# Attention into a gated FFN: the last two pairs of token tiles one after the other, stores as outputs become whole, output-weight sums and fourth sums at other places in the order

## The chip, the cores and the metric

The kernel runs on one core of one Trainium2 chip. The time is device time of one launch in microseconds (us). The core has four compute engines that matter here, each with its own instruction stream: TensorE (PE: matmuls into PSUM), VectorE (DVE), ScalarE (ACT) and GpSimd (POOL). SyncE (SP) issues most of the DMAs. An engine runs its instructions in the order in which the program was recorded and waits on semaphores for other engines.

## The reference

```python
# q, k, v: (4, 8, 768, 64); centroids: (8, 16, 64)
q_assign = argmax(q_n @ c_n.T); k_assign = argmax(k_n @ c_n.T)
mask = q_assign[..., :, None] == k_assign[..., None, :]
attn = softmax(where(mask, scale * q @ k.T, -1e9))
x = (attn @ v).transpose(0, 2, 1, 3).reshape(3072, 512)
# w_gate, w_val: (512, 1536); w_out: (1536, 512)
gate = 1.0 / (1.0 + np.exp(-(x @ w_gate)))
val = x @ w_val
return gate * val @ w_out
```

## The kernel before

The program is recorded once, in one order, by a step counter: every step is one scores block of attention (transposed keys times queries, `do_scores`, exponential on ScalarE, then `do_av`), and in between each step takes some atoms of FFN work from `queue` (`ffn_run`) and background work that was planned for that step (`plan(name, step, f)`, `at`, `run_bg`). The numbers in the table `SCHED` override the planned step where a name is in it. Batches 0 to 3 follow each other; the FFN of a block of 384 tokens runs under the attention of what comes next. The second block of the last batch has no attention to run under: `ffn_block(xT, 384, 384, B - 1, True)` and `ffn_run(1e9)` stand at the end of the program.

A block of 384 tokens is three token tiles of 128. Its FFN is 12 blocks `fc` of 128 hidden units: `gate` (L529, four matmuls, then tanh on ScalarE) and `val` (L545, four matmuls, then on VectorE `hT = (th + 1) * v`, L550). g, v, scores and most other PSUM tiles come from `ring`, four banks in turn, so a bank is free only when its reader is through. Two further banks are in the pool `op`.

For batches 1 to 3 the output product is not done tile by tile (`plain_out`) but for pairs of tiles, with seven products in place of eight (Winograd's form of a 2 by 2 product). For a pair, the hidden units are in two halves of `HF` = 6 chunks and the output columns in two halves of `HD` = 256. `tok(b, t, f)` is half f of tile t. The sums of halves are made on VectorE: on the side of the hidden units by `Sums.make(i)` (four per pair: L626 to L632), and on the side of `w_out` once by `mix_wo(i, c)` (T1 to T4, each in two halves `c`, L276), planned as `wt{i}{c}`. T1 to T3 lie in the buffers `kheld`, `qheld`, `vheld`.

`product_out` takes the products in the order 1, 4, 6, 5, 7, 3, 2 over two banks, x (1, 6, 7, 2) and y (4, 5, 3). After each, VectorE adds the bank into the output tile `ob` (`plus`, L658), with product 1 copied by ScalarE (L662). Products 7 and 3 go on accumulating in the bank that 6 and 5 filled, after the addition has read it. The fourth sum, `make(4)`, written over the second, is needed by product 3. Tiles 0, 1 of a batch are a single pair (its 14 atoms go to `aside` and alternate with those of `queue`); tiles (3, 2) and (4, 5), the second block, are two pairs at once (`P_` = 2), side by side in the columns of a bank. Each finished output row is stored by SP (`store`, L502).

In the last block the two pairs also run side by side, after all 12 gate and val blocks: six products for both, then product 2 by `closing` in three pieces.

Of the kernel before, what the change touches and what calls it, by code (L numbers as in the profile page):

```python
# [8 lines left out]
FP = mybir.dt.float32  # L9
HP = mybir.dt.float16  # L10
AF = mybir.ActivationFunctionType
ALU = mybir.AluOpType
# [86 lines left out]
def kernel(  # L99
# [61 lines left out]
    def bank(n=512, dt=FP, name="bank"):  # L161
        return ring.tile([128, n], dt, tag="ring", name=name)
# [3 lines left out]
    def out_bank():  # L166
        taken["op"] += 1
        return op.tile([128, DM], FP, tag="o", name="o")
# [103 lines left out]
    def mix_wo(i, c):  # L272
        done.add(("wt", i, c))
        o, a, z = [(T1, B12, B11), (T3, B22, B12), (T2, B22, T1), (T4, B21, T2)][i]
        c = slice(3 * c, 3 * c + 3)
        DVE.tensor_tensor(o[:, c], a[:, c], z[:, c], ALU.subtract)  # L276
# [220 lines left out]
    def tok(b, t, f):  # L497
        return HB[b, t // 3][:, HF * f : HF * f + HF, bass.ts(t % 3, 128)]

    def store(src, b, c0, n, m=slice(0, DM)):  # L500
        def f():
            SP.dma_start(  # L502
                out=out[b * S : (b + 1) * S].rearrange("(p c) m -> p c m", c=NCH)[
                    :, c0 : c0 + n, m
                ],
                in_=src,
            )

        d_ = SCHED.get("sd", 0)
        if d_ > 0 and b < B - 2:  # L510
            at(step_no[0] + d_, f)
        else:
            f()

    def ffn_atoms(xT, t0, n, b, final=False):
        blk = t0 // 384
        gv = []
        cost = NDC * max(n, 80) / 2.4 + 3
        pairs = [] if b < PB else [(0, 1)] if blk == 0 else [(3, 2), (4, 5)]
        sm = {x: Sums(b, *x) for x in pairs}  # L520

        def gate(fc, st):
            def f():
                need(("w", fc // WQ, 0), *(("x", b, p, t0 // 128 + c) for p in range(NP) for c in range(n // 128)))
                if fc == 0:
                    HB[b, blk] = htp.tile([128, NFC, 384], HP, name="hT")
                g = bank(512, name="g")
                for dc in range(NDC):
                    PE.matmul(  # L529
                        out=g[:, 0:n], lhsT=wg[fc // WQ][:, dc, fc % WQ, :],  # L530
                        rhs=xT[:, dc, t0 : t0 + n],
                        start=(dc == 0), stop=(dc == NDC - 1),
                    )
                th = thp.tile([128, 384], FP, name="th")
                ACT.activation(th[:, 0:n], g[:, 0:n], AF.Tanh)  # L535
                st.append(th)

            return f

        def val(fc, st):  # L540
            def f():
                need(("w", fc // WQ, 1))
                w = bank(512, name="v")
                for dc in range(NDC):
                    PE.matmul(  # L545
                        out=w[:, 0:n], lhsT=wv[fc // WQ][:, dc, fc % WQ, :],
                        rhs=xT[:, dc, t0 : t0 + n],
                        start=(dc == 0), stop=(dc == NDC - 1),
                    )
                DVE.scalar_tensor_tensor(  # L550
                    HB[b, blk][:, fc, 0:n], st[0][:, 0:n], 1.0, w[:, 0:n], ALU.add, ALU.mult
                )
                for k, x in SUMS_AT[b >= PB, blk].get(fc, []):
                    sm[x].make(k)
                if fc == NFC - 1 and pairs and blk == 0:
                    aside.extend(product_out(b, [sm[(0, 1)]], False))

            return f

        for fc in range(NFC):  # L560
            st = []
            gv.append((cost, gate(fc, st)))
            gv.append((cost, val(fc, st)))
        outs = []
        if b < PB:
            for t in range(n // 128):
                outs += plain_out(b, blk, t)
        elif blk == 1:
            outs = product_out(b, [sm[x] for x in pairs], final)
        return gv + outs  # L570

    def plain_out(b, blk, t):
        OA = SCHED.get(f"oa{b}{384 * blk}", SCHED.get("oa", 4))
# [33 lines left out]
        },  # L607
    }

    class Sums:  # L610


        def __init__(self, b, t1, t2):
            self.b, self.t1, self.t2, self.of = b, t1, t2, {}

        def make(self, i):
            a1 = lambda f: tok(self.b, self.t1, f)
            a2 = lambda f: tok(self.b, self.t2, f)
            if i == 4:
                self.of[4] = self.of[2]  # L620
            else:
                t = sump.tile([128, HF, 128], HP, tag="sum", name="sum")
                self.of[i] = t
            o = self.of[i]
            if i == 1:
                DVE.tensor_tensor(o, a2(0), a2(1), ALU.add)  # L626
            elif i == 2:
                DVE.tensor_tensor(o, self.of[1], a1(0), ALU.subtract)
            elif i == 3:
                DVE.tensor_tensor(o, a1(0), a2(0), ALU.subtract)  # L630
            else:
                DVE.tensor_tensor(o, a1(1), o, ALU.subtract)  # L632

    def product_out(b, sums, final):


        P_ = len(sums)
# [42 lines left out]

        def end3():
            plus(st[C12], st["y"], st[C12])
            if final:
                store(st[C12], b, sums[0].t1, P_, slice(HD, DM))

        def end2():
            plus(st[C11], st["x"], st[C11])
# [31 lines left out]

            return f  # L720

        def closing(e, a, z):
            def f():
                o = bank(z - a, name="o_end")
                lhs = tok(b, sums[e].t1, 1)
                for c in range(HF):
                    PE.matmul(  # L727
                        out=o, lhsT=lhs[:, c, :], rhs=B21[:, c, a:z],
                        start=c == 0, stop=c == HF - 1,
                    )  # L730
                m = st["o1"][:, e, a:z]
                plus(m, o, m)
                store(m.unsqueeze(1), b, sums[e].t1, 1, slice(a, z))

            return f

        for k in range(6 if final else 7):
# [3 lines left out]
        if final:  # L741
            for e, a, z in ((0, 0, HD), (1, 0, HD // 2), (1, HD // 2, HD)):
                atoms.append((900, closing(e, a, z)))
        return atoms

    queue = []
# [118 lines left out]
    def plan(name, step, f):  # L865
        at(SCHED.get(name, step), f)
# [8 lines left out]
    def need(*names):  # L875
        for n in names:
            assert n in done, n
# [623 lines left out]
```

## Time and profile before

| | us |
|---|---|
| three runs | 324.08, 324.35, 324.59 |
| the profiled execution, its own time | 324.13 |
| its span, first to last instruction | 322.3 |
| TensorE, VectorE, ScalarE, GpSimd busy | 314.6, 226.4, 231.3, 108.6 |

Rows of the profile name the line of the kernel, the engine, the operation, and the tiles written and read, with the number of instructions in a row. In the timeline the first column is the start in us from the span's start, the second the duration of the group; brackets give the idle time of that engine before it, and what ended it. The ends of matmuls are modelled and overlap the next start, so a loss on TensorE is best read from start to start. PE is TensorE's matmul, PEld its weight load, SPq SyncE's queue. The granted clock of TensorE is full over the whole span.

### The profile page before, as it was taken

Reading aid. Unit: us, or ns where it says so; the run is one execution under the profiler, and the core shown is the slowest. Engines: PE = TensorE matmul, PEld = TensorE weight load, DVE = VectorE, ACT = ScalarE, POOL = GpSimd, SP = SyncE. Lnnn points to the kernel's source line nnn. Section 1 sums busy time; section 2 is a strip of 40 time slices with the busy share of each in tenths; the row PEclk is TensorE's granted clock in tenths of the full one; section 3 lists DMA queues with packets and bytes.
Section 4 is the critical chain, followed back from the end, with each engine's and each line's share of the span. In section 5 each row is a group of like instructions: output and inputs, shape, how many; then the busy total and the mean of one; then the engine's idle time right before and its main releaser. Section 6 shows DMA issues by size and latency. Waiting matters only on the chain.

```text
span 322.3 us, 9168 instructions
## 1 busy us (share of the span) xinstructions
PE 314.6 (98%) x3510; PEld 222.1 (69%) x3510; DVE 226.4 (70%) x588; ACT 231.3 (72%) x520; POOL 108.6 (34%) x145
## 2 busy tenths in 40 slices
PE   7999999999999999999999999999999999999995
PEld 5888666766766656666777687666777688566674
DVE  5899656777667997576879588676867356555655
ACT  6688988787898977877767866788777886332220
POOL 5887464154335275433143342523111111000000
PEclk9999999999999999999999999999999999999999
DMA  6999996738988677974694652952503112200103
GB/s 205 379 253 171 259 169 120 205 85 232 248 121 226 112 218 153 229 175 130 116 212 121 202 113 60 288 124 52 111 2 91 39 26 79 77 2 1 67 0 130
DMA packets 77835, 45.15 MB, mean 140 GB/s; under 512 B 56864, under 2 KB 75232, under 8 KB 77792
## 3 DMA queue, kind: packets, MB, share of 16 engines
q1 hardware_dynamic: 73824, 39.73, 48.2%
q0 software_dynamic: 3680, 4.72, 9.0%
q8 instruction: 27, 0.44, 0.6%
q14 instruction: 16, 0.13, 0.1%
q10 hardware_dynamic: 288, 0.13, 0.1%
HBM read 28.34 MB, written 6.29 MB: 107 GB/s over the span
## 4 chain that ended last, share of the span: by engine, by line
PE 91%; DVE 6%; issue 1%; ACT 1%; ACTq 0%; POOL 0%; DVEq 0%
PE g L529 19%; PE v L545 19%; PE sc L803 18%; PE o L713 12%; PE av L826 10%; PE o L583 4%; PE lg L434 2%; PE lg L421 1%; PE t_ps L1052 1%; PE oh_ps L1112 1%; DVE lgs L449 0%; DVE T L1065 0%; DVE vheld L276 0%; PE vs_ps L354 0%; PE o_end L727 0%
## 5 line engine op out<-in xcount | busy, mean ns | idle before, releaser
L808 ACT ACTIVATE es<-sc 128x384 f16<-128x384 f32 x384 | 174.7, 492 | 40.0 <-PE sc L803 30.7
L803 PE MATMUL sc<-T 128*128 128x384 f16 x384 | 117.8, 326 | 1.0 <-DVE lgs L449 0.6
L826 PEld LDWEIGHTS <-es 128*128 128x128 f16 x1152 | 81.4, 98 | 35.3 <-issue 0.2
L826 PE MATMUL av<-va,es 128*128 128x65 f16 x1152 | 97.6, 194 | 0.0
L550 DVE SCALAR_TENSOR_TENSOR hT<-th,v 128x384 f16<-128x384 f32 x96 | 53.1, 553 | 55.8 <-PE av L826 36.6
L529 PE MATMUL g<-xTb,wg 128*128 128x384 f16 x384 | 78.2, 326 | 0.1
L545 PE MATMUL v<-xTb,wv 128*128 128x384 f16 x384 | 78.1, 326 | 0.0
L535 ACT ACTIVATE th<-g 128x384 f32<-128x384 f32 x96 | 47.2, 492 | 32.8 <-PE g L529 13.7
L375 POOL TENSOR_TENSOR xp<-t,rec 128x384 f16<-128x384 f32 (+1 forms) x30 | 21.8, 728 | 100.4 <-DVE rec L372 49.9
L529 PEld LDWEIGHTS <-wg 128*128 128x128 f16 x384 | 37.2, 97 | 19.7 <-issue 0.4
L545 PEld LDWEIGHTS <-wv 128*128 128x128 f16 x384 | 37.4, 98 | 19.0
L803 PEld LDWEIGHTS <-T 128*128 128x128 f16 x384 | 37.1, 97 | 0.7 <-DVE T L1133 0.7
L1369 POOL TENSOR_TENSOR hl<-kraw,hl 128x384 f16<-128x384 f32 x22 | 20.2, 920 | 42.0 <-DVE hl L1368 19.6
L658 DVE TENSOR_TENSOR ob<-o,ob 128x256 f32<-128x256 f32 (+1 forms) x41 | 21.9, 547 | 8.8 <-PE o L713 8.1
L713 PEld LDWEIGHTS <-sum 128*128 128x128 f16 x216 | 20.9, 98 | 5.6 <-DVE sum L632 0.7
L1369 POOL TENSOR_TENSOR hl<-qraw,hl 128x384 f16<-128x384 f32 x22 | 20.7, 940 | 10.0 <-DVE hl L1368 9.7
L713 PE MATMUL o<-wo,hT 128*128 128x256 f16 x150 | 22.5, 272 | 0.0
L370 DVE TENSOR_TENSOR t<-av,sv 128x390 f32<-128x390 f32 (+1 forms) x30 | 14.4, 479 | 8.2 <-PE av L826 7.3
L583 PE MATMUL o<-wo,hT 128*128 128x512 f16 x72 | 19.9, 379 | 0.0
L713 PEld LDWEIGHTS <-hT 128*128 128x128 f16 x150 | 14.6, 97 | 3.7
L449 DVE TENSOR_REDUCE lgs<-lg 128x192 f32<-128x384 f32 x23 | 12.7, 550 | 2.8 <-PE lg L434 2.6
L322 POOL CAST va<-vraw 128x768 f16<-128x768 f32 x15 | 13.0, 868 | 2.6 <-DMA vraw<-in_v_dram 2.6
(143 smaller groups left out, 324.9 us busy)
## 6 DMA issues: line engine op xcount, KB each, us to landing
vraw<-in_v_dram SPq DMA_DIRECT2D x15, 384.0 KB, 4.8
kraw<-in_k_dram SPq DMA_DIRECT2D x14, 384.0 KB, 4.0
out_dram<-ob SPq DMA_DIRECT2D x19, 256.0 KB, 2.3
qraw<-in_q_dram SPq DMA_DIRECT2D x12, 384.0 KB, 4.3
wg<-in_moe_w_gate_dram POOLq DMA_DIRECT2D x2, 768.0 KB, 9.6
wv<-in_moe_w_val_dram POOLq DMA_DIRECT2D x2, 768.0 KB, 10.6
wo<-in_moe_w_out_dram POOLq DMA_DIRECT2D x2, 768.0 KB, 9.3
T<-ohT SPq DMA_DIRECT2D x44, 24.0 KB, 1.9
```

Source lines behind the costliest of these rows:

```text
L375: (eng or POOL).tensor_tensor(x, t[:, 0:nq, 0:64], bcast(rec[:, 0:nq], 64), ALU.mult)
L529: PE.matmul(out=g[:, 0:n], lhsT=wg[fc // WQ][:, dc, fc % WQ, :], rhs=xT[:, dc, t0 : t0 + n], start=(dc == 0), stop=(dc == NDC - 1),)
L535: ACT.activation(th[:, 0:n], g[:, 0:n], AF.Tanh)
L545: PE.matmul(out=w[:, 0:n], lhsT=wv[fc // WQ][:, dc, fc % WQ, :], rhs=xT[:, dc, t0 : t0 + n], start=(dc == 0), stop=(dc == NDC - 1),)
L550: DVE.scalar_tensor_tensor(HB[b, blk][:, fc, 0:n], st[0][:, 0:n], 1.0, w[:, 0:n], ALU.add, ALU.mult)
L583: PE.matmul(out=o, lhsT=HB[b, blk][:, fc, bass.ts(t, 128)], rhs=wo[fc // WON][:, fc % WON, :], start=(fc == 0), stop=(fc == NFC - 1),)
L658: plus = lambda dst, a, z: DVE.tensor_tensor(dst, a, z, ALU.add)
L713: PE.matmul(out=st[z][:, e], lhsT=a[:, c, :], rhs=rhs[:, c, :], start=start and c + e == 0, stop=c == HF - 1, skip_group_check=True,)
L803: PE.matmul(out=sc.rearrange("p (c t) -> p c t", t=128), lhsT=s["k"], rhs=s["q"], start=True, stop=True,)
L808: ACT.activation(es, sc, AF.Exp, scale=SCALE)
L826: PE.matmul(out=av[:, a0 + s["c0"] + i, :], lhsT=s["es"][:, bass.ts(i, 128)], rhs=VA[b, p][:, e, s["j"], :], start=(first and i == 0 and a ...
L1369: POOL.tensor_tensor(hl[:, :, 64:128], r, hl[:, :, 0:64], ALU.subtract)
```

## The change

Three things are changed.

1. The sums of output weights: `wt0`, `wt1`, `wt2` (both halves) are planned at steps 109 to 128 instead of 150 to 170. `wt3` keeps its steps.
2. In `product_out`, the fourth sum of each pair is recorded after the addition of product 6 instead of after that of product 5.
3. The last block has an order of its own, `closing`. The first pair's products 1, 4, 6 and 5 are recorded in halves between the gate and val atoms of blocks 7 to 11. Then come product 7 of pair a, products 1 and 4 of b, 3 of a, 6 and 5 of b, 2 of a, 7 and 3 of b, and 2 of b in two column halves. Pair a uses the two banks of `op`, pair b banks of the ring. Each store follows the last addition into its part of the output. Its sums come from a table of their own, `SUMS_LAST`: those that need hidden units 6 to 11 are made in two pieces, of five chunks at block 10 and of one at block 11, and the fourth sum has its own tile.

```diff
@@ ffn_atoms
+        when = SUMS_LAST if final else SUMS_AT[b >= PB, blk]
...
-                for k, x in SUMS_AT[b >= PB, blk].get(fc, []):
-                    sm[x].make(k)
+                for k, x, *c in when.get(fc, []):
+                    sm[x].make(k, *c)
...
+        if final:
+            return closing(b, gv, sm[(3, 2)], sm[(4, 5)])
         return gv + outs
+
+    def closing(b, gv, ma, mb):
+        ac, order = [], []
+        plus = lambda dst, a, z: DVE.tensor_tensor(dst, a, z, ALU.add)
+        def pair(m, bk):
...
+            def product(k, g=0, n=HF):
+                def f():
+                    z = {1: "a", 4: "d", 6: "x", 7: "x", 5: "y", 3: "y"}[k]
...
+                    mm(o, k, g, n, k not in (7, 3))
+                    if g + n < HF:
+                        return
+                    if k == 1:
+                        ACT.activation(C(0, 0), o, AF.Copy)
+                    elif k == 4:
+                        plus(C(1, 0), o, C(0, 0))
+                    elif k == 6:
+                        plus(C(0, 1), o, C(0, 0))
+                    elif k == 5:
+                        plus(C(1, 1), o, C(0, 0))
+                    elif k == 7:
+                        plus(C(1, 0), o, C(1, 0))
+                        plus(C(1, 1), o, C(1, 1))
+                        store(st["ob"][:, 1:2], b, m.t2, 1)
+                    else:
+                        plus(C(0, 1), o, C(0, 1))
+                        store(st["ob"][:, 0:1, HD:DM], b, m.t1, 1, slice(HD, DM))
...
+            def last(parts):
+                def f():
+                    for a, z in parts:
+                        o = bank(z - a, name="o_end")
+                        mm(o, 2, 0, HF, True, a, z)
+                        plus(st["ob"][:, 0, a:z], o, st["ob"][:, 0, a:z])
+                    store(st["ob"][:, 0:1, 0:HD], b, m.t1, 1, slice(0, HD))
...
+        pa, la = pair(ma, bank_a)
+        pb, lb = pair(mb, lambda z: bank(512, name="o_end"))
+        early = [pa(k, g, HF // 2) for k in (1, 4, 6, 5) for g in (0, HF // 2)]
...
+        early[0] = drained(early[0])
+        atoms = gv[:14]
+        for i, x in enumerate(gv[14:]):
+            atoms.append(x)
+            if i < len(early):
+                atoms.append((0.0, early[i]))
+        for f in (
+            pa(7), pb(1), pb(4), pa(3), pb(6), pb(5), la([(0, HD)]), pb(7), pb(3),
+            lb([(0, HD // 2), (HD // 2, HD)]),
+        ):
+            atoms.append((0.0, f))
+        return atoms
...
+    SUMS_LAST = {
+        1: [(1, (3, 2))], 5: [(2, (3, 2)), (3, (3, 2))], 6: [(3, (4, 5))],
+        10: [(4, (3, 2), 0, 5), (1, (4, 5), 0, 5), (2, (4, 5), 0, 5), (4, (4, 5), 0, 5)],
+        11: [(4, (3, 2), 5, 6), (1, (4, 5), 5, 6), (2, (4, 5), 5, 6), (4, (4, 5), 5, 6)],
+    }
@@ product_out
         def end6():
             plus(st[C12], st["x"], st[C11])
+            for m in sums:
+                m.make(4)
 
         def end5():
             plus(st[C22], st["y"], st[C11])
-            for m in sums:
-                m.make(4)
...
@@ planned steps
-            plan(f"wt{i}{c}", (150 + 8 * i if i < 3 else 200) + 4 * c, lambda i=i, c=c: mix_wo(i, c))
+            plan(f"wt{i}{c}", (109, 118, 126, 200)[i] + (2, 2, 2, 4)[i] * c, lambda i=i, c=c: mix_wo(i, c))
```

More of the change, by code (lines that the diff above doesn't have):

```diff
@@ L614, in __init__, with make @@
             self.b, self.t1, self.t2, self.of = b, t1, t2, {}
[L616 to L624, printed above, removed]
+        def make(self, i, c0=0, c1=HF):
+            c = slice(c0, c1)
+            a1 = lambda f: tok(self.b, self.t1, f)[:, c]
+            a2 = lambda f: tok(self.b, self.t2, f)[:, c]
+            if c0 == 0:
+                if i == 4 and c1 == HF:
+                    self.of[4] = self.of[2]
+                elif i == 4:
+                    self.of[4] = tp.tile([128, 12, 128], HP, tag="T", name="T")[:, 0:HF]
+                else:
+                    self.of[i] = sump.tile([128, HF, 128], HP, tag="sum", name="sum")
+            o = self.of[i][:, c]
             if i == 1:
@@ L627, in make @@
             elif i == 2:
[L628 removed]
+                DVE.tensor_tensor(o, self.of[1][:, c], a1(0), ALU.subtract)
             elif i == 3:
@@ L631, in make, with product_out @@
             else:
-                DVE.tensor_tensor(o, a1(1), o, ALU.subtract)
-    def product_out(b, sums, final):
+                DVE.tensor_tensor(o, a1(1), self.of[2][:, c], ALU.subtract)
+    def product_out(b, sums):
         P_ = len(sums)
@@ L720, in atom @@
             return f
[L722 to L737, printed above, removed]
+        for k in range(7):
             for e in range(P_):
```

43 lines of the change are left out of this document (36 added, 7 removed).

## The prediction

> **What bounds the kernel now.** I read the page first, then the starts of the matmuls one by one, then the queues of the engines that a late matmul waited for.
>
> ```profile
> span 322.3 us, 9168 instructions
> ...
> PE 314.6 (98%) x3510; PEld 222.1 (69%) x3510; DVE 226.4 (70%) x588; ACT 231.3 (72%) x520; POOL 108.6 (34%) x145
> ...
> PE 91%; DVE 6%; issue 1%; ACT 1%; ACTq 0%; POOL 0%; DVEq 0%
> ```
>
> TensorE is busy 98% of the span and is 91% of the chain that ended last. The change keeps every matmul, so it can only win where TensorE waits and after its last matmul. I price the three such places that it touches.
>
> *Place 1, at 115 us.* The timeline of TensorE (start, duration, what ran, idle time before it and its releaser):
>
> ```profile
> 112.94 0.45 PE L434 MATMUL lg<-cm,T 128*128 128x32 f16 x12
> ...
> 114.12 0.25 PE L826 MATMUL av<-va,es 128*128 128x65 f16 x3
> 114.21 0.32 PE L803 MATMUL sc<-T 128*128 128x384 f16 x1
> ...
> 114.81 0.25 PE L826 MATMUL av<-va,es 128*128 128x65 f16 x3
> 115.63 0.32 PE L803 MATMUL sc<-T 128*128 128x384 f16 x1 [0.57 <-DVE lgs L449]
> ```
>
> And that of VectorE:
>
> ```profile
> 113.14 1.08 DVE L276 TENSOR_TENSOR vheld<-wo,wo 128x768 f16<-128x768 f16 x1
> 114.14 0.98 DVE L1368 CAST hl<-qraw 128x384 f16<-128x384 f32 x1
> 115.04 0.54 DVE L449 TENSOR_REDUCE lgs<-lg 128x192 f32<-128x384 f32 x1
> ```
>
> Three av matmuls take 0.09 us from start to start (114.12 to 114.21), so the scores after 114.81 were due at 114.90 and came at 115.63: 0.73 us lost. They needed the PSUM bank that the reduction lgs empties. That reduction had its input at 113.39 (112.94 + 0.45) and started at 115.04, behind half a sum of output weights (L276) and a cast.
>
> *Place 2, the two-pair product of batch 1, at 195 us.* TensorE, then VectorE:
>
> ```profile
> 195.23 0.49 PE L713 MATMUL o<-vheld,sum 128*128 128x256 f16 x3
> 195.94 0.50 PE L713 MATMUL o<-wo,sum 128*128 128x256 f16 x3 [0.22 <-DVE sum L632]
> ...
> 200.65 0.95 PE L529 MATMUL g<-xTb,wg 128*128 128x384 f16 x4
> ```
>
> ```profile
> 191.31 0.69 DVE L658 TENSOR_TENSOR ob<-o,ob 128x512 f32<-128x512 f32 x1 [0.48 <-PE o L713]
> ...
> 194.73 0.68 DVE L658 TENSOR_TENSOR ob<-o,ob 128x512 f32<-128x512 f32 x1
> 195.33 1.02 DVE L632 TENSOR_TENSOR sum<-hT,sum 128x768 f16<-128x768 f16 x2
> 196.26 1.28 DVE L658 TENSOR_TENSOR ob<-o,ob 128x512 f32<-128x512 f32 x2
> ```
>
> Three matmuls of 256 columns take 0.33 us (0.11 each: 72 of them run from 308.90 to 316.87, below), so the product with the fourth sum was due at 195.56 and lost 0.38 us. From the addition at 191.31, which follows the sixth product, to the sums, no VectorE row shows idle time before it. So here VectorE's whole queue is late, not the one sum.
>
> *Place 3, the end.* TensorE, VectorE, SP's queue, and the landing of single stores (size, us):
>
> ```profile
> 302.40 0.81 PE L529 MATMUL g<-xTb,wg 128*128 128x384 f16 x4
> ...
> 308.25 0.81 PE L545 MATMUL v<-xTb,wv 128*128 128x384 f16 x4
> 308.90 2.78 PE L713 MATMUL o<-wo,hT 128*128 128x256 f16 x24
> ...
> 316.87 1.49 PE L727 MATMUL o_end<-wo,hT 128*128 128x256 f16 x18
> ```
>
> ```profile
> 309.17 0.55 DVE L550 SCALAR_TENSOR_TENSOR hT<-th,v 128x384 f16<-128x384 f32 x1 [0.75 <-PE v L545]
> ...
> 318.40 0.29 DVE L658 TENSOR_TENSOR ob<-o_end,ob 128x128 f32<-128x128 f32 x1
> ```
>
> ```profile
> 317.19 2.85 SPq L502 DMA_DIRECT2D out_dram<-ob  x6
> ...
> 319.63 0.40 SPq L502 DMA_DIRECT2D out_dram<-ob  x1
> ```
>
> ```profile
> out_dram<-ob SPq DMA_DIRECT2D x1, 256.0 KB, 2.0
> ...
> out_dram<-ob SPq DMA_DIRECT2D x1, 128.0 KB, 2.4
> ...
> out_dram<-ob SPq DMA_DIRECT2D x1, 64.0 KB, 1.7
> ```
>
> The last result is in SBUF at 318.69 (318.40 + 0.29), but its store is issued at 319.63: six stores stand in SP's queue from 317.19 on, one each 0.49 us ((319.63 - 317.19) / 5). The last one, of 64 KB, lands at 321.3; 1.0 us of closing follows to 322.3. So the end is bound by the issue of stores, 0.94 us behind the last result. The 128 KB row is the store before the last two, with others on both sides; the 256 KB row is one that had the queue to itself.
>
> **The change, part by part.**
>
> *Output-weight sums at steps 109 to 128 instead of 150 to 170.* Six of the eight leave the stretch from 105 to 119 us. Without the one at 113.14, the cast and lgs move up: lgs starts behind a cast of at most 0.98 that can now begin near 112.6, runs 0.54 and is done by about 114.1, before 114.90. Gain 0.73, and the chain runs through TensorE from there to the end, so nothing fills the hole. In the built order the six now stand among these rows:
>
> ```profile
> 83.13 0.19 DVE L372 RECIPROCAL rec<-t 128x6 f32<-128x6 f32 x1
> 83.49 0.55 DVE L550 SCALAR_TENSOR_TENSOR hT<-th,v 128x384 f16<-128x384 f32 x1 [0.16 <-PE av L826]
> ...
> 86.06 0.55 DVE L550 SCALAR_TENSOR_TENSOR hT<-th,v 128x384 f16<-128x384 f32 x1 [1.34 <-PE v L545]
> ...
> 88.74 0.55 DVE L550 SCALAR_TENSOR_TENSOR hT<-th,v 128x384 f16<-128x384 f32 x1 [0.59 <-PE av L826]
> ...
> 91.06 0.55 DVE L550 SCALAR_TENSOR_TENSOR hT<-th,v 128x384 f16<-128x384 f32 x1 [1.06 <-PE av L826]
> ...
> 93.74 0.56 DVE L550 SCALAR_TENSOR_TENSOR hT<-th,v 128x384 f16<-128x384 f32 x1 [1.65 <-PE av L826]
> ```
>
> TensorE and GpSimd beside them, and two more sums of before, one beside GpSimd's xp:
>
> ```profile
> 84.47 0.33 PE L803 MATMUL sc<-T 128*128 128x384 f16 x1
> ```
>
> ```profile
> 83.41 0.82 POOL L375 TENSOR_TENSOR xp<-t,rec 128x384 f16<-128x384 f32 x1 [2.49 <-PE v L545]
> ...
> 111.56 0.98 POOL L375 TENSOR_TENSOR xp<-t,rec 128x384 f16<-128x384 f32 x1 [4.99 <-PE sc L803]
> ```
>
> ```profile
> 105.72 1.27 DVE L276 TENSOR_TENSOR kheld<-wo 128x768 f16<-128x768 f16 x1
> ...
> 111.34 0.52 DVE L276 TENSOR_TENSOR vheld<-wo,wo 128x768 f16<-128x768 f16 x1
> ```
>
> The first stands behind the reciprocal at 83.13, the second behind the hidden update at 83.49, the next two on either side of the update at 88.74, the last two behind that at 91.06. The first ends near 83.8 and puts off the update of 83.49 until about 84.35, when the scores at 84.47 need its bank: 0.1 us to spare. The second fits the 1.34 us idle before 86.06, the third the 0.59 before 88.74, the fourth the 1.06 before 91.06, the last two the 1.65 before 93.74. Queued behind the second are two casts for a later head, and behind the fourth an av evacuation, 0.5 us later, with that idle time after it. I take 0. The bounds are 0, at 0.52 each, and 0.6: two of them at 1.27 less the slack of their place, some 0.3 each. The cover is VectorE's idle time; without it the scores at 84.47 wait.
>
> A rule speaks against this edit. By the Trainium skill (SBUF — State Buffer, Who interferes with whom), a VectorE instruction with two SBUF inputs contends with a GpSimd instruction that reads SBUF, and whichever issues first keeps the shared ports until it is through. The trace agrees: the sum at 111.34 came ahead of xp and kept its 0.52, while xp stretched to 0.98 from 0.82. The first moved sum is also next in line after a reciprocal that xp waits for, so by the rule it goes first again; were it second, the third rival would follow.
>
> *A pair's fourth sum after the sixth product's addition instead of the fifth's.* For single pairs, whose product comes two turns later, it costs nothing either way, and in batch 2 VectorE idles around it. At place 2 it costs. The two sums (0.93 from 195.33 to 196.26) now stand ahead of everything between the additions of 191.31 and 194.73, so the fifth product's addition ends at 195.41 + 0.93 = 196.34. The product with the fourth sum writes on in the bank that this addition reads, so it waits until about 196.41 instead of 195.94: 0.47 more. Before, it needed that addition and the first sum only. Of this, 0.14 is not paid, because the gate at 200.65 (0.95 instead of 0.81) waits for a transposed tile whose VectorE work is no later than it was. Net +0.33; bounds 0 (the delay is swallowed) and 0.5.
>
> *The closing, TensorE.* Pair a's first four products go in halves (0.33 each) between the five last gate and val blocks (0.65 each, (308.90 - 302.40) / 10), so the last val ends at 308.90 + 8 x 0.33 = 311.54. The other 66 matmuls end at the old time unless one waits.
>
> *The closing, VectorE.* It now makes eight part sums at blocks 10 and 11, which no row shows. For one 640 wide I take 0.46 to 0.56, from the 0.52 and 0.55 of whole sums and updates, and choose 0.49; for one 128 wide at most 0.29 (the row at 318.40), and 0.2. The update of block 10 starts 0.92 after its val (309.17 - 308.25), at 310.18; four wide sums and one addition follow; the update of block 11 ends near 313.5. Pair b's fourth product needs it for its sixth matmul at 311.54 + 17 x 0.109 = 313.39: some 0.15 lost, nearly what the old end lost to its late sums. TensorE's end stays. Two more waits I exclude: the first early product takes the bank that the older pair's third product has left, emptied one product earlier, and the last products find theirs free.
>
> *The closing, stores.* Three of the six now go before pair b's seventh product, which TensorE ends at 311.54 + 8 x 0.655 + 0.15 = 316.93. Its two additions (about 0.42 each, between the 0.29 of 128 columns and the 0.69 of 512) end near 317.9. The stores follow at 317.95, 318.44 and 318.93 instead of 319.63: 0.70 earlier. But the last is 128 KB, not 64. It lands after 2.0, as the lone 256 KB store does (bounds 1.7 and 2.4), at 320.93 instead of 321.3: gain 0.4, bounds 0 and 0.7.
>
> **Sum.** -0.73 + 0 + 0.33 - 0.4 = -0.8. The profiled execution took 324.13 us, its span of 322.3 and 1.8 around it; the sum makes it 323.3. The median of the runs shown, 324.35, lies 0.2 above it, and on that scale, used below, the forecast is 323.6.
>
> **The rivals.**
>
> *One: the fourth sums cost nothing at place 2,* as the edit means it. For it: the gate at 200.65 already waits for a transfer, so a delay before it may be swallowed. Against it: VectorE's rows there have no hole. -0.73 - 0.4 = -1.1: 323.2.
>
> *Two: the end gains nothing.* A 128 KB store that takes 2.4, as quoted, lands at 321.33. Then -0.73 + 0.33 = -0.4: 323.95, which is no change that can be told. Against it: that store shared the queue with over 0.5 MB.
>
> *Three, slower: the moved weight sums come second to GpSimd.* If they take 1.27 instead of 0.52, TensorE waits 0.65 at 84.47 (0.75 less the 0.1 to spare) and 0.75 for the update of 86.06, whose slack the two casts behind the second sum use up, at 0.98 each as at 114.14; 0.6 more comes from the two sums around 88.74, whose slack of 0.59 covers half. 2.0 in all: -0.8 + 2.0 = +1.2: 325.5. It decides itself where xp of 83.41 starts ahead of the first sum; the row at 111.34 speaks against it, that at 105.72 for it.
>
> **How the numbers follow.** Forecast 0.50, rival one 0.22, two 0.18, three 0.10. A measurement of this kernel can tell about 0.2% from no change, 0.65 us, so faster means below 323.7. The forecast lies 0.1 below that; by its bounds I count three quarters of it as faster: 0.38 + 0.22 = 0.60. Same: 0.12 + 0.18 = 0.30. Slower: 0.10. The range runs from the best bounds (-0.73 + 0 - 0.7: 322.9) to the second rival with place 2 at 0.5 and one crowded weight sum (323.95 + 0.17 + 0.3 = 324.4); rival three stays outside.
>
> **What would show it.** No wait for lgs near 115; weight sums (L276) near 83 to 93 at 0.5 to 0.6 us with no TensorE wait beside them; a longer wait of the product with the fourth sum near 195, now for an addition (ob) instead of a sum; a short wait for hT near 313; the last store issued some 0.2 after the last addition instead of 0.94. The forecast is wrong if TensorE waits near 84 or 86, if the wait near 195 is gone, or if the last store still lands 2.6 after the last addition.

## The result, and the profile after

| | us |
|---|---|
| before, six runs beside the changed kernel | 324.3 (324.08 to 324.59) |
| changed, six runs | 323.09 (322.67 to 323.67) |
| ratio | 0.9959, 95% interval 0.9944 to 0.9974 |
| changed, profiled execution, its own time (span) | 323.67 (321.9) |

The change makes the kernel 0.41% faster, 1.2 us by the medians, where 0.8 was forecast; 323.6 was forecast and 323.09 came, inside the range. The profiled execution is the slowest of its six. Its span is only 0.4 below that of before, so the two traces show where time moved, and the runs of the experiments say how much of it stays.

The page of the changed kernel, its head and the shares of its chain:

```profile
span 321.9 us, 9181 instructions
...
PE 314.6 (98%) x3510; PEld 222.4 (69%) x3510; DVE 224.9 (70%) x598; ACT 231.1 (72%) x521; POOL 108.6 (34%) x145
...
PE 89%; DMA 3%; DVE 3%; issue 2%; POOL 1%; SPq 0%; ACT 0%; POOLq 0%; DVEq 0%
```

TensorE does the same 3510 matmuls in the same 314.6 us. DMA has come into the chain with 3%: TensorE now waits at some places for a transposed tile.

*Place 1, near 115 us.* The timeline of TensorE, then of VectorE (start, duration, what ran):

```profile
114.99 0.25 PE L916 MATMUL av<-va,es 128*128 128x65 f16 x3
115.08 0.33 PE L893 MATMUL sc<-T 128*128 128x384 f16 x1
```

```profile
112.86 0.82 DVE L1458 CAST hl<-qraw 128x384 f16<-128x384 f32 x1
113.64 0.56 DVE L449 TENSOR_REDUCE lgs<-lg 128x192 f32<-128x384 f32 x1
```

From av to the scores it is 0.09 us again; the 0.73 of before is gone. The reduction lgs starts at 113.64 instead of 115.04, since the half sum of weights that stood at 113.14 is no longer ahead of the cast.

*Where the weight sums went.* VectorE between 83 and 94 us, then TensorE, then GpSimd:

```profile
83.28 0.52 DVE L276 TENSOR_TENSOR kheld<-wo 128x768 f16<-128x768 f16 x1
...
89.25 0.55 DVE L276 TENSOR_TENSOR vheld<-wo,wo 128x768 f16<-128x768 f16 x1
89.72 0.56 DVE L370 TENSOR_TENSOR t<-av,sv 128x390 f32<-128x390 f32 x1
...
92.51 1.07 DVE L276 TENSOR_TENSOR qheld<-wo,kheld 128x768 f16<-128x768 f16 x1
```

```profile
84.42 0.26 PE L916 MATMUL av<-va,es 128*128 128x65 f16 x3
84.51 0.33 PE L893 MATMUL sc<-T 128*128 128x384 f16 x1
```

```profile
83.45 1.04 POOL L375 TENSOR_TENSOR xp<-t,rec 128x384 f16<-128x384 f32 x1 [2.50 <-PE v L546]
...
90.58 0.82 POOL L375 TENSOR_TENSOR xp<-t,rec 128x384 f16<-128x384 f32 x1 [3.45 <-DVE rec L372]
92.00 1.16 POOL L1459 TENSOR_TENSOR hl<-qraw,hl 128x384 f16<-128x384 f32 x1 [0.59 <-DVE hl L1458]
```

The scores at 84.51 follow the av matmuls after 0.09 us: no wait there. But the half sum at 89.25 stands ahead of the evacuation t and the reciprocal (89.72; before 89.21), so xp comes at 90.58 instead of 90.08. SP's queue shows what that carries with it, changed and then before:

```profile
91.44 1.21 SPq L947 DMA_TRANSPOSE xTb<-xp  x1
...
94.51 1.70 SPq L410 DMA_TRANSPOSE T<-hl  x1
```

```profile
90.93 1.21 SPq L857 DMA_TRANSPOSE xTb<-xp  x1
...
94.00 1.40 SPq L410 DMA_TRANSPOSE T<-hl  x1
```

SP runs in order: the transpose of xp waits for xp, then comes one of ohT, and behind it the transpose T of a later head's keys and queries. T's own input is ready long before (hl, 92.00 + 1.16 = 93.16), yet it goes out at 94.51 instead of 94.00. TensorE's blocks there start 0.05 later than before, so against them T is issued 0.46 later. The assignment scores lg that read T then wait; TensorE of the changed kernel:

```profile
99.02 0.26 PE L916 MATMUL av<-va,es 128*128 128x65 f16 x3
99.41 0.47 PE L434 MATMUL lg<-cm,T 128*128 128x32 f16 x12
```

They were due at 99.11 and lose 0.30; before, by the same count, 0.13. It is 0.17 more and not 0.46, because T landed 4.8 us after its issue here and 5.1 before.

*Place 2, near 195 us.* VectorE, then TensorE:

```profile
191.37 1.01 DVE L742 TENSOR_TENSOR sum<-hT,sum 128x768 f16<-128x768 f16 x2
...
195.05 1.88 DVE L768 TENSOR_TENSOR ob<-o,ob 128x512 f32<-128x512 f32 x3
```

```profile
194.68 0.49 PE L821 MATMUL o<-vheld,sum 128*128 128x256 f16 x3
195.78 0.49 PE L821 MATMUL o<-wo,sum 128*128 128x256 f16 x3 [0.62 <-DVE ob L768]
...
200.48 0.65 PE L530 MATMUL g<-xTb,wg 128*128 128x384 f16 x3
201.68 0.32 PE L530 MATMUL g<-xTb,wg 128*128 128x384 f16 x1 [0.54 <-DMA xTb<-xp]
```

The two sums run at 191.37, and the addition of the fifth product does not start until 195.05. The product with the fourth sum was due at 195.01 (194.68 + 0.33) and came at 195.78: 0.77 lost, against 0.38, and what it waited for is an addition (ob) instead of a sum. The gate's fourth matmul, due at 200.97, comes 0.71 late; before it was 0.14.

*Place 3, the end.* VectorE, TensorE, the last store on SP's queue, and its landing (KB, us):

```profile
313.34 0.54 DVE L551 SCALAR_TENSOR_TENSOR hT<-th,v 128x384 f16<-128x384 f32 x1
...
318.86 0.29 DVE L580 TENSOR_TENSOR ob<-o_end,ob 128x128 f32<-128x128 f32 x1
```

```profile
312.57 1.65 PE L594 MATMUL o_end<-wo,hT 128*128 128x256 f16 x12
314.06 0.82 PE L594 MATMUL o<-wo,T 128*128 128x256 f16 x6
```

```profile
319.23 0.40 SPq L502 DMA_DIRECT2D out_dram<-ob  x1
```

```profile
out_dram<-ob SPq DMA_DIRECT2D x1, 128.0 KB, 1.8
```

Twelve matmuls of 0.109 from 312.57 end their turn at 313.88; the next starts at 314.06, so 0.18 is lost waiting for the update of 313.34. The last addition ends at 319.15, the last store is issued at 319.23, 0.08 behind it instead of 0.94. It lands 1.76 us later (1.8 in the row), at 320.99; 0.91 of closing follows.

The windows of the last microseconds show the transfers, before first (second number the window's length; last two columns: mean busy share of the 16 DMA engines, which can pass 1 at a window's edge, and GB/s):

```profile
318.00:319.00 1.00, 0.36 (x7) 0.19 (x4) 0.65 (x3) 0.00 (x0) 0.00 (x0) 1.00 0.99 379
319.00:320.00 1.00, 0.00 (x0) 0.00 (x0) 0.00 (x0) 0.00 (x0) 0.00 (x0) 1.00 1.07 390
320.00:321.00 1.00, 0.00 (x0) 0.00 (x0) 0.00 (x0) 0.00 (x0) 0.00 (x0) 1.00 0.88 280
```

```profile
318.00:319.00 1.00, 0.82 (x14) 0.65 (x11) 0.96 (x4) 0.00 (x0) 0.00 (x0) 1.00 0.38 131
319.00:320.00 1.00, 0.00 (x0) 0.00 (x0) 0.15 (x1) 0.00 (x0) 0.00 (x0) 1.00 0.86 328
320.00:321.00 1.00, 0.00 (x0) 0.00 (x0) 0.00 (x0) 0.00 (x0) 0.00 (x0) 1.00 0.57 197
```

Before, all 16 DMA engines are full from 318 to nearly 321: the whole 1.05 MB of the last six stores leaves in that stretch, about 2.8 us at 380 GB/s. In the changed kernel half of it has left by 319 (328 and 197 KB of the 1049 come after), and only then comes a stretch near full.

*The traces side by side.* TensorE's losses differ by -0.73 at 115, +0.17 at 99, +0.39 at 195, +0.57 at the gate and +0.07 at the update near 314 (0.11 before, of another kind): +0.47 together. TensorE's last matmul ends at 318.82 instead of 318.36, the 0.46 that makes. From there to the end of the span it is 3.07 instead of 3.98: -0.91. Together -0.45, what the spans differ by. So all that this one execution wins, it wins at the end; the gain at 115 has been lost again, half of it to the gate's transposed tile.

### The profile page after: what moved, and what is told of

Read it like the earlier page. It is cut to its first block, busy times and chain, and to the rows that moved or that the text cites. A ratio compares the mean times of both kernels' runs of the same rounds, so it can differ in the third digit from the quotient of the medians.

```text
span 321.9 us, 9181 instructions
## 1 busy us (share of the span) xinstructions
PE 314.6 (98%) x3510; PEld 222.4 (69%) x3510; DVE 224.9 (70%) x598; ACT 231.1 (72%) x521; POOL 108.6 (34%) x145
## 4 chain that ended last, share of the span: by engine, by line
PE 89%; DMA 3%; DVE 3%; issue 2%; POOL 1%; SPq 0%; ACT 0%; POOLq 0%; DVEq 0%
PE g L530 19%; PE v L546 19%; PE sc L893 17%; PE av L916 10%; PE o L821 8%; PE o L684 5%; PE lg L434 2%; PE o_end L594 2%; DMA T<-hl 2%; PE lg L421 1%; PE t_ps L1142 1%; PE o L594 1%; DMA xTb<-xp 1%; PE oh_ps L1202 1%; DMA qraw<-in_q_dram 1%
## 5 line engine op out<-in xcount | busy, mean ns | idle before, releaser
L768 DVE TENSOR_TENSOR ob<-o,ob 128x256 f32<-128x256 f32 (+1 forms) x35 | 17.8, 523 | 7.6 <-PE o L821 6.8
L821 PEld LDWEIGHTS <-sum 128*128 128x128 f16 x168 | 16.4, 98 | 5.2 <-issue 0.8
L821 PE MATMUL o<-wo,hT 128*128 128x256 f16 x126 | 19.8, 272 | 0.0
L821 PEld LDWEIGHTS <-hT 128*128 128x128 f16 x126 | 12.2, 97 | 3.4
```

The costliest lines, as they stand in the source:

```text
L768: plus = lambda dst, a, z: DVE.tensor_tensor(dst, a, z, ALU.add)
L821: PE.matmul(out=st[z][:, e], lhsT=a[:, c, :], rhs=rhs[:, c, :], start=start and c + e == 0, stop=c == HF - 1, skip_group_check=True,)
```

## The experiments

Each kernel ran in several rounds beside the kernel before, on one chip within a group; 324.2 to 324.3 is the kernel before in all three groups. Times are medians, ratios have their 95% interval, and differences in us are the ratio's.

**The three parts alone.** `e1_weights` is the kernel before with the weight sums moved and nothing else.

```diff
-            plan(f"wt{i}{c}", (150 + 8 * i if i < 3 else 200) + 4 * c, lambda i=i, c=c: mix_wo(i, c))
+            plan(f"wt{i}{c}", (109, 118, 126, 200)[i] + (2, 2, 2, 4)[i] * c, lambda i=i, c=c: mix_wo(i, c))
```

> The kernel before with the sums of output weights alone moved to steps 109 to 128. Theory: the wait for lgs near 115 us goes (0.73 us) and nothing comes near 83 to 93: 0.7 us below before, ratio 0.998. Rival three (the sums wait behind GpSimd there): above before. Rival (the freed time is taken by a later wait): within 0.2 us of before.

323.73, ratio 0.9985 (0.9974 to 0.9996): -0.49 us instead of -0.73. The wait at 115 is gone and none stands near 84 or 86, but lg near 99 waits. TensorE of this kernel:

```profile
98.79 0.26 PE L826 MATMUL av<-va,es 128*128 128x65 f16 x3
99.58 0.46 PE L434 MATMUL lg<-cm,T 128*128 128x32 f16 x12 [0.53 <-DMA T<-hl]
```

Due at 98.88, it comes at 99.58: 0.70 lost, 0.57 more than before. Against TensorE's matmuls T is issued 0.47 later, and that much comes from the sums; the other 0.1 is its transfer, 5.2 us from issue to landing instead of 5.1. How much of the late issue TensorE pays differs between executions. T is issued at the same point of TensorE's work, within 0.01 us, in all five profiles with the sums where they were, and some 0.47 later in all seven with the half sum of 89.25 ahead of the evacuation. The waits at 99 are 0 to 0.38 in the first (0.38 in `e5_two_queues`) and 0 to 0.70 in the second, 0.10 and 0.36 on average; so the sums cost some 0.25 there, an estimate from these twelve traces.

`e2_fourth` is the kernel before with the fourth sums moved and nothing else.

```diff
         def end6():
             plus(st[C12], st["x"], st[C11])
+            for m in sums:
+                m.make(4)
 
         def end5():
             plus(st[C22], st["y"], st[C11])
-            for m in sums:
-                m.make(4)
```

> The kernel before with the fourth sums alone moved from behind product 5's addition to behind product 6's. Theory: the wait of the product with the fourth sum in batch 1 grows from 0.38 to about 0.8 us and ends at an addition: 0.2 to 0.5 us above before, ratio 1.001. Rival one (the move costs nothing or gains the 0.38): equal to before or up to 0.4 us below.

324.73, ratio 1.0012 (1.0003 to 1.0021): +0.39 us, slower. Its product with the fourth sum, on TensorE:

```profile
195.69 0.49 PE L713 MATMUL o<-vheld,sum 128*128 128x256 f16 x3
196.80 0.49 PE L713 MATMUL o<-wo,sum 128*128 128x256 f16 x3 [0.62 <-DVE ob L658]
```

0.78 lost (196.80 less 196.02) where it was 0.38, for the addition. The first rival, that this edit costs nothing, falls for the kernel before; this part of the change is a loss by itself.

`e3_closing` is the kernel before with the new closing and nothing else (against the changed kernel, the two other edits are taken back).

```diff
         def end6():
             plus(st[C12], st["x"], st[C11])
-            for m in sums:
-                m.make(4)
 
         def end5():
             plus(st[C22], st["y"], st[C11])
+            for m in sums:
+                m.make(4)
...
-            plan(f"wt{i}{c}", (109, 118, 126, 200)[i] + (2, 2, 2, 4)[i] * c, lambda i=i, c=c: mix_wo(i, c))
+            plan(f"wt{i}{c}", (150 + 8 * i if i < 3 else 200) + 4 * c, lambda i=i, c=c: mix_wo(i, c))
```

> The kernel before with the last block's own order alone (fourth sums of the other pairs and sums of weights as before). Prediction: 0.4 us below before. Theory since the result: the last store is issued 0.8 us nearer to TensorE's last matmul and lands within 1.8 us: 0.8 us below before, ratio 0.9975. Rival two (the end gains nothing): equal to before.

323.57, ratio 0.9976 (0.9961 to 0.9990): -0.78 us, the largest of the three. The second rival, no gain at the end, falls, and the forecast's 0.4 is too small. Its last store also lands 1.77 after its issue. The three parts alone sum to -0.49 + 0.39 - 0.78 = -0.88.

**The change without its loss.** `e4_no_fourth` is the changed kernel with only the fourth sums back behind the fifth product.

```diff
         def end6():
             plus(st[C12], st["x"], st[C11])
-            for m in sums:
-                m.make(4)
 
         def end5():
             plus(st[C22], st["y"], st[C11])
+            for m in sums:
+                m.make(4)
```

> The changed kernel with the fourth sums of the pairs in product_out back behind product 5's addition. Theory: 0.2 to 0.5 us below the changed kernel (323.1), so 322.6 to 322.9, ratio to before 0.9952; the wait near 195 us is 0.38 again and ends at a sum. Rival one: equal to the changed kernel or above it.

323.17, ratio 0.9968 (0.9955 to 0.9980). A miss: it should have come 0.4 below the changed kernel and did not, though the wait at 195 is back at 0.38 (for the sum). In its profile the gate near 200.5 loses 0.61 for the transposed tile. The interval of 0.4 us to either side leaves room for the 0.4 as well, so the times decide nothing. The traces show one way in which the gain can go: in the profile of `e11_changed_again`, the changed kernel once more, that tile lands 3.1 us after its issue and here 3.0, place 2 loses 0.78 there and 0.38 here, and the gate 0.23 there and 0.61 here. Between these two executions the gate takes back all that place 2 gains, as the first rival has it.

**What bounds the end.** `e5_two_queues` is the kernel before with three of the last six stores issued by ScalarE, so that no store waits its turn.

```diff
-    def store(src, b, c0, n, m=slice(0, DM)):
+    def store(src, b, c0, n, m=slice(0, DM), q=None):
...
-            SP.dma_start(
+            (q or SP).dma_start(
...
-                store(st["o2"][:, i], b, m.t2, 1)
+                store(st["o2"][:, i], b, m.t2, 1, q=ACT if final and i else None)
...
-                store(m.unsqueeze(1), b, sums[e].t1, 1, slice(a, z))
+                store(m.unsqueeze(1), b, sums[e].t1, 1, slice(a, z), q=ACT if e == 0 or a == 0 else None)
```

> The kernel before, with three of its last six stores issued by ScalarE's queue instead of SP's; nothing else changed. Theory (the end is bound by one store after the other on SP's queue): the last store is issued within 0.2 us of the last addition instead of 0.94, the end is 0.6 to 0.9 us sooner, ratio 0.9977. Rival (the transfers themselves bind the end, 1 MB in the last microseconds): the last store lands no sooner, 0 to 0.2 us below before.

324.66, ratio 1.0016 (1.0007 to 1.0024): slower by 0.52 us. A clear miss for the step that the issue of stores alone sets the end. The last store on SP's queue, its issue, and its landing (KB, us), then the windows:

```profile
318.71 0.33 SPq L502 DMA_DIRECT2D out_dram<-ob  x1
```

```profile
out_dram<-ob SPq DMA_DIRECT2D x1, 64.0 KB, 2.9
```

```profile
318.00:319.00 1.00, 0.32 (x6) 0.14 (x3) 0.60 (x3) 0.00 (x0) 0.00 (x0) 1.00 1.02 389
319.00:320.00 1.00, 0.00 (x0) 0.00 (x0) 0.00 (x0) 0.00 (x0) 0.00 (x0) 1.00 1.05 380
```

The last store goes out 0.92 earlier than before (318.71 against 319.63), 0.06 behind the last addition, and lands 2.9 us later instead of 1.7. The engines are full over the same stretch as before: whoever issues them, the same bytes go through the same 16 engines. By the Trainium skill (DMA: Bandwidth & Descriptors, Issuing engines are not separate DMA queues), starting DMAs on several engines saves only the time to initiate them; the windows agree. That the end came 0.5 later is more than the rule says, and why is open.

`e10_few_bytes` is the kernel before with its last six stores in the old order, but each writes only the first 32 of its columns; the rest of those rows is left out.

```diff
-    def store(src, b, c0, n, m=slice(0, DM)):
+    def store(src, b, c0, n, m=slice(0, DM), few=False):
+        if few:
+            src, m = src[..., 0:32], slice(m.start, m.start + 32)
...
-                store(st["o2"][:, i], b, m.t2, 1)
+                store(st["o2"][:, i], b, m.t2, 1, few=final)
...
-                store(st[C12], b, sums[0].t1, P_, slice(HD, DM))
+                store(st[C12], b, sums[0].t1, P_, slice(HD, DM), True)
...
-                store(m.unsqueeze(1), b, sums[e].t1, 1, slice(a, z))
+                store(m.unsqueeze(1), b, sums[e].t1, 1, slice(a, z), True)
```

> The kernel before, with each of the last six stores writing only the first 32 of its columns (the rest of these outputs is left out): as many stores, a sixth or less of the bytes. If the order on SP's queue binds the end, the last store is still issued 0.9 us after the last addition and the end moves by 0 to 0.2 us. If the transfers bind it, stores land within 1.7 us and the end is 0.5 us or more sooner although the issue is where it was.

323.85, ratio 0.9987 (0.9976 to 0.9999): -0.42 us. The last store on SP's queue and the window:

```profile
318.72 0.38 SPq L505 DMA_DIRECT2D out_dram<-ob  x1
```

```profile
318.00:319.00 1.00, 0.00 (x0) 0.00 (x0) 0.15 (x1) 0.00 (x0) 0.00 (x0) 1.00 0.32 49
```

With a tenth of the bytes the engines are idle two thirds of this time, yet the last store still goes out 0.57 behind the last addition (318.72 against 318.15), for SP issues the last four one each 0.47 to 0.50. From TensorE's end (317.83) to the span's end it is 3.36, against 3.98 before and 3.07 in the changed kernel: 0.62 less than before.

That is not the worth of the bytes alone, since the edit relieves SP's queue too. The 32 columns that the first two stores write are whole after the first of product 7's two additions, so the first store goes out at 316.06, 1.77 before TensorE's end; before, it was 317.19, 1.17 before the end. The last store follows TensorE's end by 0.89 instead of 1.27. This earlier issue is 0.38 of the 0.62; the shorter landing, 1.45 instead of 1.67, is 0.22. So neither of the two expected outcomes came as stated, and fewer bytes behind an unchanged queue were not tried. What the two runs show together: an earlier issue of all the bytes wins nothing (`e5_two_queues`), and an earlier issue of a tenth of them shortens the end. Transfers and queue both hold it, within some 0.2 us of each other as an estimate from that landing. The closing relieves both, since half the bytes and half the issues are through before the last products.

**What makes the wait at 99.** `e6_behind_rec` is `e1_weights` with one of the six half sums, that of 89.25, one step later, behind the reciprocal.

```diff
-            plan(f"wt{i}{c}", (109, 118, 126, 200)[i] + (2, 2, 2, 4)[i] * c, lambda i=i, c=c: mix_wo(i, c))
+            plan(f"wt{i}{c}", (109, 118, 126, 200)[i] + (2, 3, 2, 4)[i] * c, lambda i=i, c=c: mix_wo(i, c))
```

> The kernel before with the weight sums at steps 109 to 128 as in e1_weights, but the fourth half sum one step later, so that it stands behind the av evacuation and its reciprocal instead of ahead of them. Theory (the evacuation was 0.47 us late, and through xp and SP's queue so were the transposes of the next keys): the transpose that TensorE waits for at 99 us is issued 0.4 to 0.5 us sooner, that wait falls from 0.70 to 0.1 to 0.2 us, and the whole is 0.3 to 0.5 us below e1_weights (323.73): 323.2 to 323.4. Rival (the wait at 99 us comes from the two casts behind the second sum, or from slower transfers): the wait and the time as in e1_weights.

323.54, ratio 0.9980 (0.9969 to 0.9991), 0.16 better than `e1_weights`, which the intervals don't tell apart. Against TensorE's matmuls, the transpose of T is issued 0.21 later than before, where `e1_weights` has 0.47, and the wait at 99 is 0.33 instead of 0.70. The direction is as expected, the size half. The other 0.21 comes from the same half sum: in its new place, at 89.89 behind the reciprocal, it runs beside GpSimd's xp, which takes 1.04 from 90.05 on instead of 0.82.

`e9_one_half` asks the converse: the kernel before with that one half sum alone moved to the step that it has in the changed kernel.

```diff
-            plan(f"wt{i}{c}", (150 + 8 * i if i < 3 else 200) + 4 * c, lambda i=i, c=c: mix_wo(i, c))
+            plan(f"wt{i}{c}", 120 if (i, c) == (1, 1) else (150 + 8 * i if i < 3 else 200) + 4 * c, lambda i=i, c=c: mix_wo(i, c))
```

> The kernel before with one half sum of output weights alone (the fourth) moved to step 120, where it stands ahead of the av evacuation near 89 us; the other five stay at 105 to 119 us. Theory (this half sum is what made the transposes of the next keys late in e1_weights): they are issued about 0.47 us later measured from TensorE's work, the wait at 99 us grows to 0.5 to 0.7, the wait at 115 stays: 0.2 to 0.5 us above before, ratio 1.001. Rival (the wait at 99 us moves with the transfers from run to run): a wait as in the kernel before, and its time.

324.23, ratio 1.0003 (0.9991 to 1.0014). The transpose of T is issued 0.47 later, as in the changed kernel, and TensorE waits for it twice:

```profile
98.46 0.26 PE L826 MATMUL av<-va,es 128*128 128x65 f16 x3
98.95 0.47 PE L434 MATMUL lg<-cm,T 128*128 128x32 f16 x12 [0.23 <-DMA T<-hl]
...
120.43 0.26 PE L826 MATMUL av<-va,es 128*128 128x65 f16 x3
121.19 0.47 PE L434 MATMUL lg<-cm,T 128*128 128x32 f16 x12 [0.51 <-DMA T<-hl]
```

0.40 and 0.67 are lost. What was not expected is that the wait at 115 went too. It should have been: this half sum is the one that stood at 113.14, directly ahead of the cast and lgs. So one of the six takes the whole 0.73, and here gives it back, 0.27 more at 99 and 0.67 at 121. The late issue shows that this half sum alone delays T. The second wait is another matter: the T that is read there is issued 5.17 ahead of its due time, against 5.36 in the kernel before, but lands 5.8 us after its issue instead of 3.8. Why that transfer took longer is open.

**A better place for the fourth sums.** `e7_in_place` is the changed kernel with those of `product_out` written over the first half of the second tile, which no product reads, and made behind products 1 and 4, where VectorE is not behind.

```diff
-                    self.of[4] = self.of[2]
+                    self.of[4] = tok(self.b, self.t2, 0)
...
+            sums[0].make(4)
...
+            for m in sums[1:]:
+                m.make(4)
...
         def end6():
             plus(st[C12], st["x"], st[C11])
-            for m in sums:
-                m.make(4)
```

> The changed kernel with the fourth sums of the pairs in product_out made earlier still, behind the first and fourth products, where VectorE has idle time; they are written over the first half of the pair's second tile, which no product reads. Theory: the wait near 195 us (0.78) is gone, and the gate near 200 us waits less too, since VectorE's queue is shorter: 0.5 to 0.9 us below the changed kernel (323.09), 322.2 to 322.6. Rival (the gate near 200 us waits for its transposed tile all the same and takes the gain): 323.0.

322.48, ratio 0.9951 (0.9939 to 0.9963): -1.59 us. `e8_both` adds the shift of `e6_behind_rec` to it.

```diff
-            plan(f"wt{i}{c}", (109, 118, 126, 200)[i] + (2, 2, 2, 4)[i] * c, lambda i=i, c=c: mix_wo(i, c))
+            plan(f"wt{i}{c}", (109, 118, 126, 200)[i] + (2, 3, 2, 4)[i] * c, lambda i=i, c=c: mix_wo(i, c))
```

> e7_in_place with the fourth half sum of weights behind the reciprocal as in e6_behind_rec. Theory: both gains together, 0.3 to 0.5 us below e7_in_place, 321.8 to 322.2, ratio to before 0.993. Rival (one wait takes the place of the other): as e7_in_place.

322.69, ratio 0.9955 (0.9939 to 0.9970): no gain over `e7_in_place`, a miss. Its profiled execution, the slowest of its eleven, waits 1.16 for a transposed T near 122. That T is issued as far ahead of its due time as in the changed kernel (5.68 and 5.69 us) but lands 6.8 instead of 4.7 us after its issue; that the shift moved the wait there is not shown.

To compare the best kernel and the changed one on one chip, both ran once more.

> The changed kernel once more, on the chip of the other runs of this group, to compare e12 with: 323.1, ratio 0.996. The wait at the gate near 200 us, 0.7 in its first profile, should be another one here (0 to 0.5) if it comes from how long the transposing transfer takes in that run.

> e7_in_place once more beside the changed kernel: 0.4 to 0.8 us below it if the 0.78 us wait near 195 us is what the early fourth sums take away; equal to it if the gate near 200 us takes the gain.

The changed kernel: 323.4, ratio 0.9974 (0.9961 to 0.9986), -0.84 us. The kernel of `e7_in_place`: 322.46, ratio 0.9947 (0.9930 to 0.9964), -1.72 us, 0.9 below it and below the kernel before. Its VectorE and TensorE at place 2:

```profile
187.28 0.52 DVE L742 TENSOR_TENSOR hT<-hT,sum 128x768 f16<-128x768 f16 x1
```

```profile
194.18 0.49 PE L822 MATMUL o<-vheld,sum 128*128 128x256 f16 x3
194.58 0.49 PE L822 MATMUL o<-wo,hT 128*128 128x256 f16 x3
```

The product that lost 0.77 now follows within 0.07 of its due time (194.51). The first sum, at 187.28, costs VectorE 0.52; the second, at 189.22, even 0.88, but they end 6.8 and 4.5 us ahead of that product.

## Why the prediction was right, and where not

**Place 1: right.** The wait for lgs is gone from the traces above of the kernels that moved the sums, and `e9_one_half` shows that the half sum of 113.14 alone made it.

**The moved weight sums at nothing: wrong.** The failed step is "behind the fourth an av evacuation, 0.5 us later, with that idle time after it. I take 0." The evacuation was 0.5 late as said, and VectorE did have idle time after it. But the step stopped at VectorE. Behind the evacuation stand GpSimd's xp, SP's transpose of xp, and then, because SP issues in order, the transpose of the next T, which TensorE needs near 99. It cost 0.17 in the profiled execution of the changed kernel and 0.57 in that of `e1_weights`. By the runs the whole edit is worth -0.49 instead of -0.73, so 0.2, inside the bounds of 0 to 0.6 but by a path they had not named; the interval, -0.84 to -0.13, does not exclude -0.73, so it is the traces that show the loss. `e9_one_half` shows the half sum as the cause of T's late issue.

The rest of that part held. The first sum kept 0.52 and ended at 83.80, no TensorE wait stood at 84 or 86, and the third rival (sums second to GpSimd) did not come, though two of the six took longer than the 0.5 to 0.6 that was expected: 0.72 at 84.18 and 1.07 at 92.51. The trace agrees twice with the rule of the Trainium skill (SBUF — State Buffer, Who interferes with whom): the sum at 83.28 issued first and kept 0.52, while xp beside it took 1.04 instead of 0.82; the last sum, at 92.51, issued behind hl (92.00) and took 1.07, where idle time covers it. What it would cost where none does was not tried.

**The fourth sums: right in the kernel before, size included.** +0.33 was forecast, from a wait grown by 0.47 that ends at an addition; it grew by 0.39 and ends there, and `e2_fourth` measures +0.39. The 0.14 that the gate was to swallow cannot be seen: the gate lost 0.71 in this execution, 0.23 in that of `e11_changed_again`, 0.61 in that of `e4_no_fourth`. How long the transposed tile took from issue to landing, in the changed kernel and in the kernel before:

```profile
xTb<-xp SPq DMA_TRANSPOSE x1, 3.6
```

```profile
xTb<-xp SPq DMA_TRANSPOSE x1, 2.6
```

In `e11_changed_again`, the same program as the first, it took 3.1. A slack of 0.14 behind such a transfer was no firm term, and `e4_no_fourth` leaves open how much of the 0.39 the changed kernel pays.

**The closing: the mechanism right, the size too small, and one reason wrong.** -0.4 was forecast, -0.78 measured alone. The profile gives the terms, counted from TensorE's end: the last store is issued 0.41 behind it instead of the forecast 0.57 (before 1.27), it lands after 1.76 instead of 2.0, and the closing after it takes 0.91 instead of 1.04. TensorE's own part was near: 0.18 lost for the late update where 0.15 was forecast. Of the 0.53 that these terms come out shorter, the landing makes the largest part, 0.24. The 0.13 of closing is not the change's: it is 0.92 in the profile of `e1_weights` as well, which has the old end, and from TensorE's end to the span's end that profile has 3.87. So the gain at the end is 0.8 to 0.9 by the traces. 2.0 was taken from a lone 256 KB store, with 1.7 as the low end; a 128 KB store behind two others took 1.76, near the 64 KB store of before.

The failed reason is "So the end is bound by the issue of stores, 0.94 us behind the last result." The rows show that queue, but not that it is the only bound: `e5_two_queues` removes it and is slower. The 16 DMA engines were full for about 2.8 us, which a window over the last microseconds would have shown on the profile of before. The forecast gained from the right edit for half of the right reason.

**The sum.** -0.8 was forecast; the parts alone sum to -0.88 by the runs, and the two measurements of the changed kernel, -1.33 (-1.82 to -0.84) and -0.84 (-1.26 to -0.45), hold it. The first median lies nearest to the first rival's 323.2, but in `e2_fourth` the 0.39 that this rival denies is paid, and the closing's larger gain makes up for it. Two errors, 0.2 lost at 99 and 0.4 won at the end, partly cancelled; that the sum came so near the measured parts is in part luck.

## What to carry to other kernels

When an instruction is put into an engine's idle time, follow its delay through every queue behind it to the next reader on the bounding engine, in-order DMA queues included; idle time on the engine itself is not enough. Before calling a tail bound by the issue of stores, look at the share of the DMA engines in that stretch: where they were full, as here, a second queue did not help, and bytes had to leave earlier. A sum that competes with late additions is best moved to where its engine is not behind, even if it needs another buffer: that took the wait of 0.77 away that moving it by one addition had only doubled.

## What the runs showed that was not expected

- Two issuing queues for the last stores: landings of 2.5 to 3.3 us instead of 1.7 to 2.4, and 0.16% slower (0.07 to 0.24), with the engines equally full.
- The transposing DMAs that TensorE waits for vary from one execution to the next: from 2.5 to 3.6 us for xTb near 200, 4.5 to 5.4 us for T near 95, among kernels that differ in nothing there or little. That spread is as large as the terms of this sum, so a single profile can hide a gain of 0.7 us, as that of the changed kernel did.
- A store of 128 KB behind two others on one queue lands in 1.76 us, one of 16 KB in `e10_few_bytes` in 1.45: 16 or 128 KB made 0.3 of difference.
